# Half of two DRAM streams moved to GpSimd's queue, and a new order of the work, in a tuned Fourier filter with a gated convolution

## The chip, the cores and the metric

The kernel runs on one core of one Trainium2 chip. The metric is the device time in microseconds (us): the median of three runs is 857.64 us (857.32 to 858.21). The changed kernel is compared with the kernel before on the same chip. Inside the core, TensorE (PE in the profile) does the matrix products, VectorE (DVE) and ScalarE (ACT) do the element-wise work, SyncE (SP) issues nearly all transfers, and GpSimd (POOL) is almost unused before the change.

## The reference

```
x: (8, 3200, 256)
X  = rfft(x, axis=1)
Yr = X.real @ w_r - X.imag @ w_i + b_r
Yi = X.real @ w_i + X.imag @ w_r + b_i
Yr, Yi = soft-threshold of both by 0.01       # sign(Y) * max(|Y| - 0.01, 0)
y  = irfft(Yr + 1j*Yi, n=3200, axis=1)        # (8, 3200, 256)
gate_pre[s] = sum over k < 5 of conv_w[k] * y[s - 4 + k]   # causal, per channel
out = (sigmoid(gate_pre) * (y @ w_val)) @ w_out
```

The three convolution matrices (`moe_w_val`, `moe_conv_w`, `moe_w_out`) arrive as 64-bit floats or as 32-bit ones; here the kernel holds code that turns 64-bit words into 32-bit floats on VectorE.

## The kernel before, in words

The transform of 3200 points is split into 64 x 50 points, forwards and backwards. One batch (of eight) goes through five stages:

1. **p1**, the first transform: eight units `u`. A unit reads eight of the 64 columns of x as two halves of a tile (`half(0)`, rows 0 to 49, and `half(1)`, rows 64 to 113), makes four or five products into `p` (L594, L599, L601), copies one half to SBUF on ScalarE (L607) and makes sum and difference with the other half on VectorE (`fold`, L613). `store` writes the result `s` to the scratch `a_dram` in DRAM (L554 through `by_rows`, L631 for one column of unit 0).
2. **p2**: blocks `d` of four frequencies each are read back from `a_dram` (`a`, L650), transformed again (`s`, L668), split into high and low parts (`xs`, L713 to L721), multiplied with the complex weights (`y_ps`, L782 and L786, with the bias seed on ScalarE, L764, and a bias step on VectorE, L788, between the two), soft-thresholded (`tp`, L794 and L796), transformed back (`z_ps`, L737) and written to `z_dram` (L753).
3. **positions**: eight groups read `z_dram` (`zl`), make the last transform (`y_p`, L848) and put y into `y_sb`; when group 1 is there, a small copy (L866) joins the ends of the sequence.
4. **conv**: ScalarE makes the first tap (L896), VectorE the other four (`acc`, L899), ScalarE the sigmoid (L909).
5. **gated**: the value product (`v_ps`), the gating (L933), the output product (`o_ps`), and the store to `out` (L960). The big products are made of three matmuls on a high and a low part each (L882); the last ones of the run use whole 32-bit words instead (L878).

The stages of neighbouring batches overlap: p1 of batch b+1 runs beside p2 of batch b and the positions, conv and gated work of batch b-1. `a_dram` exists twice, so p2 of a batch starts only when all its stores have landed.

**What sets the order.** The program is not written in the order in which it runs. `Plan.add` collects pieces with an engine, a cost and a key `at`; `Plan.order` then plays them on one queue per engine and, among the pieces that could begin at about the same time, takes the one with the smallest `at`. The keys are `batch * 13 + unit` plus offsets from the table `O`, one offset per kind of piece. The planner knows transfers by their kilobytes only: one common wire of `WIRE` bytes per ns, a lag `LANDED` and a `BACKLOG`. The result is a fixed list of instructions for each engine. Every engine and every queue works its list strictly in order.

**Queues.** `QUEUES` names SyncE and ScalarE; ScalarE's queue is used only for one half of x in the first two units of batch 0. All else (1001 transfers in the list) is SyncE's. A transfer of 50 rows is issued as two (`ROWS`: 48 rows and 2 rows). A queue has eight completion counters that it uses in turn, so a transfer waits for the one eight places before it on the same queue.

**Idle TensorE.** Before real work is there, TensorE runs products that nobody reads (`warm`, L987, and `zeros`, L363).

## Time and profile before

| | |
|---|---|
| median of three runs | 857.64 us |
| the profiled execution's own time | 859.73 us |
| span from its first to its last instruction | 857.8 us |
| mean granted TensorE clock | 0.973 of full |
| PE busy | 821.0 us, 96% |
| DVE busy | 736.2 us, 86% |
| ACT busy | 593.7 us, 69% |
| POOL busy | 4.5 us, 1% |
| transfers | 162.27 MB in 125909 packets, mean 189 GB/s |

Busy shares are means over stages with different limits. TensorE's matmuls overlap, so a busy TensorE is not TensorE at its peak. In the rows further down a line begins with either a stretch of time or a source line; a value in square brackets, or behind a second bar, is idle time of the engine just before and what ended it. "PEclk" is the TensorE clock that was granted, as a share of its full speed, and "DMA share" the mean busy share of the 16 DMA engines. The first positions group of batch 0, which opens the steady part of the run, begins at 152.8 us.

### The profile page before, as it was taken

How to read it: one execution, taken by the hardware profiler on the slowest of the kernel's cores; microseconds unless marked ns; L12 is line 12 of the kernel's file. 1: busy time of each engine (PE TensorE's matmuls, PEld its weight loads, DVE VectorE, ACT ScalarE, POOL GpSimd, SP SyncE). 2: the span in 40 equal slices, each digit the busy share in tenths (PEclk: the TensorE clock that was granted, in tenths of full speed). 3: DMA queues.
4: the chain of work that ended last, by engine and by line, in shares of the span. 5: the costliest groups of instructions: out<-in, count | busy, mean ns of one | idle time of the engine just before them, and what ended most of it. 6: DMA issues, size and time to landing. Idle time of an engine off the chain costs nothing.

```text
span 857.8 us, 23810 instructions
## 1 busy us (share of the span) xinstructions
PE 821.0 (96%) x9866; PEld 700.7 (82%) x9866; DVE 736.2 (86%) x1006; ACT 593.7 (69%) x903; POOL 4.5 (1%) x12
## 2 busy tenths in 40 slices
PE   8878867999999999999999999999999999999997
PEld 2456656889888988889988989899888999998874
DVE  3345679799998999899989998999989998998795
ACT  2234635778777786778777886878777787776753
POOL 0000000000000000000000000000001000000000
PEclk7888979999999999999999999999999999999999
DMA  6688889867886569776796759876895576225422
GB/s 169 182 190 224 246 214 250 228 179 191 209 234 185 165 180 258 203 204 174 224 245 195 192 175 248 206 206 187 231 234 158 157 200 193 71 83 173 133 76 96
DMA packets 125909, 162.27 MB, mean 189 GB/s; under 512 B 12528, under 2 KB 100234, under 8 KB 125802
## 3 DMA queue, kind: packets, MB, share of 16 engines
q1 hardware_dynamic: 125598, 160.34, 68.1%
q8 instruction: 78, 1.28, 0.7%
q10 hardware_dynamic: 204, 0.41, 0.2%
q14 instruction: 29, 0.24, 0.1%
HBM read 82.06 MB, written 78.64 MB: 187 GB/s over the span
## 4 chain that ended last, share of the span: by engine, by line
PE 69%; DVE 13%; DMA 9%; ACT 4%; SPq 3%; issue 2%; DVEq 0%; ACTq 0%
PE o_ps L882 13%; PE y_ps L782 12%; PE v_ps L882 11%; PE y_p L848 10%; PE y_ps L786 6%; DMA x<-in_x 4%; PE p L594 4%; PE s L668 4%; PE z_ps L737 4%; DVE acc L899 4%; PE v_ps L878 2%; SPq L554 2%; DMA zl<-z_dram 1%; DVE acc L933 1%; DVE gated L390 1%
## 5 line engine op out<-in xcount | busy, mean ns | idle before, releaser
L899 DVE SCALAR_TENSOR_TENSOR acc<-y_sb,cw_sb,acc 128x800 f32<-128x800 f32 x256 | 263.0, 1047 | 16.1 <-ACT acc L896 15.6
L782 PEld LDWEIGHTS y_ps<-w_sb,xs 128*128 128x128 f32 x1152 | 144.3, 191 | 28.4 <-DVE y_ps L788 12.4
L782 PE MATMUL y_ps<-w_sb,xs 128*128 128x256 f32 x1152 | 156.3, 286 | 11.1 <-DVE y_ps L788 11.0
L882 PE MATMUL o_ps<-gated,wo_sb 128*128 128x400 f32 x744 | 150.8, 349 | 0.8 <-DVE gated L390 0.8
L882 PEld LDWEIGHTS o_ps<-gated,wo_sb 128*128 128x128 f32 x744 | 134.6, 188 | 4.1 <-DVE gated L390 1.1
L882 PE MATMUL v_ps<-y_hl,wv_sb 128*128 128x400 f32 x648 | 128.4, 346 | 0.5 <-DVE s L613 0.5
L882 PEld LDWEIGHTS v_ps<-y_hl,wv_sb 128*128 128x128 f32 x648 | 115.4, 188 | 1.1 <-PE y_ps L786 0.7
L613 DVE TENSOR_TENSOR s<-p,s 128x512 f32<-128x512 f32 (+2 forms) x144 | 89.3, 626 | 27.5 <-ACT s L607 16.4
L848 PEld LDWEIGHTS y_p<-g_sb,zl 100*64 100x64 f32 x2048 | 89.1, 137 | 11.7 <-ACT y_ps L764 3.5
L848 PE MATMUL y_p<-g_sb,zl 100*64 100x100 f32 x2048 | 97.4, 251 | 0.7 <-DMA zl<-z_dram 0.5
L786 PE MATMUL y_ps<-w_sb,xs 128*128 128x256 f32 x576 | 90.0, 293 | 7.6 <-ACT y_ps L764 7.6
L786 PEld LDWEIGHTS y_ps<-w_sb,xs 128*128 128x128 f32 x576 | 79.3, 194 | 20.9 <-ACT y_ps L764 9.0
L794 ACT ACTIVATE tp<-y_ps,nlam 128x512 f32<-128x512 f32 (+1 forms) x104 | 70.0, 674 | 25.1 <-PE y_ps L782 25.1
L388 ACT CAST gated<-acc 128x800 fp32r<-128x800 f32 x62 | 53.3, 859 | 30.7 <-DVE acc L933 30.5
L601 PE MATMUL p<-x,f_sb 50*64 50x512 f32 x240 | 72.2, 654 | 1.7 <-DMA x<-in_x 1.7
L933 DVE TENSOR_TENSOR acc<-v_ps,acc 128x800 f32<-128x800 f32 x64 | 62.9, 984 | 11.4 <-PE v_ps L878 5.5
L796 DVE SCALAR_TENSOR_TENSOR tp<-y_ps,tp 128x512 f32<-128x512 f32 (+1 forms) x104 | 68.6, 661 | 4.1 <-ACT tp L794 4.0
L594 PE MATMUL p<-x,f_sb 50*64 50x512 f32 x256 | 71.6, 647 | 0.1
L668 PEld LDWEIGHTS s<-f_sb,a 64*64 64x64 f32 x3072 | 53.7, 137 | 19.5 <-issue 11.6
L909 ACT ACTIVATE acc<-acc 128x800 f32<-128x800 f32 x64 | 55.8, 878 | 16.3 <-DVE acc L899 16.0
L958 ACT COPY o<-o_ps 128x800 f32<-128x800 f32 x63 | 51.8, 822 | 21.3 <-PE o_ps L882 15.8
L716 DVE TENSOR_TENSOR sx<-s,sx 128x512 f32<-128x512 f32 x48 | 33.0, 688 | 38.2 <-ACT xs L713 37.2
(92 smaller groups left out, 1031.3 us busy)
## 6 DMA issues: line engine op xcount, KB each, us to landing
out<-o SPq DMA_DIRECT2D x126, 200.0 KB
a<-a_dram SPq DMA_DIRECT2D x96, 256.0 KB
z_dram<-z_t SPq DMA_DIRECT2D x48, 512.0 KB
zl<-z_dram SPq DMA_DIRECT2D x64, 384.0 KB
a_dram<-s SPq DMA_DIRECT2D x120, 192.0 KB
x<-in_x SPq DMA_DIRECT2D x119, 192.0 KB
a_dram<-s SPq DMA_DIRECT2D x120, 8.0 KB
x<-in_x SPq DMA_DIRECT2D x119, 8.0 KB
```

The costliest lines, as they stand in the source:

```text
L594: nc.tensor.matmul(p[k * HP:(k + 1) * HP, 0, :], f1_sb[half(0), 0:HP], xt[half(0), k * 512:(k + 1) * 512], start=True, stop=True)
L601: nc.tensor.matmul(dst, f1_sb[half(1), 0:HP], back[:, 2 * k:2 * k + 2, :], start=True, stop=True)
L613: nc.vector.tensor_tensor(out=st()[lo:hi, h, n], in0=tl[kp][lo:hi, 0, n], in1=st()[lo:hi, 1, n], op=(ALU.add, ALU.subtract)[h])
L668: nc.tensor.matmul(p[e * HP:(e + 1) * HP, h, c, t, :], tl[ka][rows, t, c * P + e * HP:c * P + (e + 1) * HP], f2_sb[rows, (4 * d + t) * N1: ...
L782: nc.tensor.matmul(p[:, 1 - r, :], xm(hx, c, r, i), w_sb[:, m, hw, c, :], start=False, stop=k == 5, skip_group_check=True)
L786: nc.tensor.matmul(tl[ky][:, 0], sm(hx, c, i), w_sb[:, 0, hw, c, :], start=False, stop=k == 5, skip_group_check=True)
L794: nc.scalar.activation(out=buffer(kt, "tp", [P, 2, D])[:, 0:n], in_=tl[ky][:, 0:n], func=AF.Relu, bias=nlam)
L796: add(at + 0.2, "DVE", dve(n * D), lambda: nc.vector.scalar_tensor_tensor(out=tl[kt][:, 0:n], in0=tl[ky][:, 0:n], scalar=LAM, in1=tl[kt][: ...
L848: nc.tensor.matmul(dst[e * HP:(e + 1) * HP], zt[0:Q, m, c * P + e * HP:c * P + (e + 1) * HP], g, start=True, stop=True)
L882: nc.tensor.matmul(p[:, e, 0:TB], w[:, hw, c, e * P:(e + 1) * P], src(hy, c), start=n == 0, stop=n == 5)
L899: nc.vector.scalar_tensor_tensor(out=acc(c), in0=wide(c, j), scalar=cw_sb[:, c, j:j + 1], in1=acc(c), op0=ALU.mult, op1=ALU.add)
L933: add(at + O["gate"], "DVE", dve(2 * TB), lambda: nc.vector.tensor_tensor(out=part(), in0=by_half(tl[kv][:, :, 0:TB]), in1=part(), op=ALU. ...
```

## The change

Three things change together.

- **Queues.** `QUEUES` is now SyncE and GpSimd. In every unit of p1 of every batch, half 0 of x is loaded by SyncE and half 1 by GpSimd. `store` is cut into two pieces `k` of four columns each: piece 0 goes by SyncE and piece 1 by GpSimd, except in units 5 to 7 of batch 0, where both go by SyncE. SyncE's list shrinks from 1001 transfers to 717, GpSimd's grows from none to 274 (144 for x, 130 for `a_dram`), ScalarE's six go.
- **Layout.** A row of `a_dram` was one frequency of one fold (100 rows: first all sums, then all differences). Now a row is a frequency (50 rows) with the sum and the difference of each column side by side, and the SBUF tile `s` has the same order, so that a store moves rows of 1024 words in one piece where before it moved two runs of 512 words. The column of unit 0 that is written with its folds exchanged takes two transfers instead of four. The reads of `a` keep runs of 256 words.
- **Order.** The planner gets a model of the eight counters of a queue (`lanes`), other constants and a newly searched table `O`. Every engine's list is in a new order. The memsets on GpSimd that nobody needs at once are put behind the first ones.

```diff
+        lanes, turn = {e: [0.0] * 8 for e in (False, True)}, {False: 0, True: 0}
+        def lane(p):
+            row, at = lanes[p["engine"] == "POOL"], turn[p["engine"] == "POOL"]
+            return max([row[(at + j) % 8] - 350 * j for j in range(lanes_of(p))], default=0.0)
...
-WIRE = 250
+WIRE = 260
 BACKLOG = 5000
-LANDED = 2500
+LANDED = 2200
+SOFT = 1500
...
-     'p3': 1.0966,
-     'conv': 25.53,
+     'p3': 9.2044,
+     'conv': 42.5736,
...
-    QUEUES = (("SP", nc.sync), ("ACT", nc.scalar))
-    BOTH = 2
+    QUEUES = (("SP", nc.sync, 700), ("POOL", nc.gpsimd, 1040))
...
+        first = -100 + u if early else at + O["load_x"] + O["load_x_1"] * (b == 1)
+        for g, (eng, queue, cost) in enumerate(QUEUES):
+            add(first + 0.001 * g, eng, cost, lambda g=g, queue=queue: load(g, queue), (),
+                [kx + (g,)], None if g else {kx: x_tag}, kb=200, chain="x" + eng, extra=SOFT * g)
...
-        st = lambda: tl[ks].rearrange("p (h n) -> p h n", h=NH)
+        st = lambda: tl[ks].rearrange("p (m h c) -> p h m c", h=NH, c=D)
...
-        def store():
+        def store(k, queue):
+            if u == k == 0:
+                buffer(ka, "a_dram", [N2, NM * 2 * D])
+            lo = (2 * u + k) * 4 * D
+            n = 2 * D if lo == 0 else 0
+            by_rows(queue, tl[ka][:, lo + n:lo + 4 * D], tl[ks][k * HP:k * HP + N2, n:], rows)
             if u == 0:
-                buffer(ka, "a_dram", [Q, NM * D])
-            dst = tl[ka].rearrange("(h f) mc -> f h mc", h=NH)
-            for k in range(2):
-                lo = u * 4 * D + k * 512
-                n = D if lo == 0 else 0
-                by_rows(nc.sync, dst[:, :, lo + n:lo + 512], st()[k * HP:k * HP + N2, :, n:], rows)
-            if u == 0:
-                for g in range(NH):
-                    for r in range(2):
-                        nc.sync.dma_start(out=dst[r::2, g, 0:D], in_=st()[r:N2:2, 1 - g if r else g, 0:D])
+                both = lambda ap: ap.rearrange("f (h c) -> f h c", h=NH)
+                queue.dma_start(out=both(tl[ka][k::2, 0:2 * D]), in_=both(tl[ks][k:N2:2, 0:2 * D])[:, ::1 - 2 * k])
+        for k, (eng, queue, cost) in enumerate(QUEUES[:1] * 2 if early and u > 4 else QUEUES):
...
-            src = tl["a_dram", b].rearrange("(h f) (m c) -> h (f m) c", h=NH, c=D)
+            src = tl["a_dram", b].rearrange("f (m h c) -> h (f m) c", h=NH, c=D)
```

**Where the order changes, first place.** SyncE's list of the kernel before, from the last stores of batch 0 to the first read of `a` and what follows (`s1_254` is unit 7's folded tile, `x_296` unit 0 of batch 1; 1024 words are one row of a half):

```order
L554 DMA a_dram_168<-s1_254 48x2x512
L554 DMA a_dram_168<-s1_254 2x2x512
L490 DMA g1_sb_70<-in_g1 128x256
L650 DMA a_293<-a_dram_168 64x4x256 x2
L554 DMA x_296<-in_x 48x1024
L554 DMA x_296<-in_x 2x1024
L554 DMA x_296<-in_x 48x768
L554 DMA x_296<-in_x 2x768
```

SyncE's list of the changed kernel at the same place (`s1_253` is unit 7, `x_297` and `x_302` are units 1 and 2 of batch 1; unit 0 of batch 1 stands still earlier, ahead of all stores):

```order
L568 DMA a_dram_175<-s1_253 48x1024
L568 DMA a_dram_175<-s1_253 2x1024
L568 DMA x_297<-in_x 48x1024
L568 DMA x_297<-in_x 2x1024
L568 DMA x_302<-in_x 48x1024
L568 DMA x_302<-in_x 2x1024
L504 DMA g1_sb_70<-in_g1 128x256
L499 DMA f2_sb_68<-in_f2 128x256
L658 DMA a_309<-a_dram_175 64x4x256 x2
L658 DMA a_312<-a_dram_175 64x4x256 x2
```

Three units of batch 1's x and a further part of the matrix `f2` now stand ahead of the first read of `a`, and the second read follows the first at once. In GpSimd's list 18 transfers of batch 0's x (half 1 of eight units) and 11 stores (units 0 to 4) come before its three units of batch 1.

**Second place.** TensorE's list of the kernel before, around the point where VectorE turns `moe_w_val` into 32-bit words (`p_1042` is unit 0 of batch 2; the conversion's 13 VectorE instructions stand between that unit's folds and the bias step that releases the third row from the bottom):

```order
L786 MATMUL y_ps<-w_sb,xs 128x256 x6
L594 MATMUL p_1042<-x,f_sb 64x512 x2
L599 MATMUL p_1042<-x,f_sb 64x256 x2
L601 MATMUL p_1042<-x,f_sb 64x512
L782 MATMUL y_ps<-w_sb,xs 128x256 x12
L786 MATMUL y_ps<-w_sb,xs 128x256 x6
L782 MATMUL y_ps<-w_sb,xs 128x256 x12
L786 MATMUL y_ps<-w_sb,xs 128x256 x6
L737 MATMUL z_ps<-tp,g_sb 64x256 x8
```

TensorE's list of the changed kernel around the same conversion (`p_1061` and `p_1073` are units 0 and 1 of batch 2; the conversion stands before the bias step that releases the `x12` row under them):

```order
L794 MATMUL y_ps<-w_sb,xs 128x256 x6
L603 MATMUL p_1061<-x,f_sb 64x512 x2
L608 MATMUL p_1061<-x,f_sb 64x256 x2
L610 MATMUL p_1061<-x,f_sb 64x512
L603 MATMUL p_1073<-x,f_sb 64x512 x2
L610 MATMUL p_1073<-x,f_sb 64x512 x2
L790 MATMUL y_ps<-w_sb,xs 128x256 x12
L794 MATMUL y_ps<-w_sb,xs 128x256 x6
L745 MATMUL z_ps<-tp,g_sb 64x256 x8
```

Two units of p1 now stand between the sums and the product that waits for the conversion, and their folds come behind the conversion on VectorE and not ahead of it.

**In numbers, over the whole lists.** The count of matmuls that are used stays the same on every line; those that nobody reads fall from 26 to 22 (`zeros`), with 13 `warm` ones in both. TensorE goes between 64-column and full tiles 192 times before and 204 times after. Behind the last threshold step of the run (L796, now L804), VectorE has 42 taps, 13 gatings and 12 splits left before, and 56, 16 and 18 after. Behind the last `y_ps` product, TensorE has 36 more `v_ps`, 36 more `o_ps` matmuls and three more `y_p` groups left than before.

## Rows read from the trace of the kernel before

**Rows 1.** Busy time in stretches of the start, all engines (window, share; clock, DMA)
```profile
0.00:21.00 21.00, 17.59 (x54) 4.92 (x58) 7.68 (x13) 4.66 (x8) 1.29 (x10) 0.71 0.69 170
21.00:41.00 20.00, 19.56 (x84) 10.27 (x84) 8.23 (x14) 5.72 (x11) 0.00 (x0) 0.88 0.69 192
41.00:70.00 29.00, 20.25 (x306) 14.58 (x306) 12.69 (x21) 9.52 (x16) 0.00 (x0) 0.88 0.82 188
70.00:95.00 25.00, 21.90 (x265) 16.34 (x258) 13.82 (x21) 13.39 (x22) 0.00 (x0) 0.86 0.88 236
...
116.00:137.00 21.00, 20.61 (x276) 16.10 (x280) 16.49 (x41) 13.31 (x23) 0.00 (x0) 0.87 0.94 250
```

**Rows 2.** The same view of the steady part and of the end
```profile
153.00:753.00 600.00, 597.90 (x7833) 538.63 (x7830) 564.07 (x750) 467.65 (x711) 3.26 (x2) 1.00 0.72 197
...
774.00:858.00 84.00, 78.19 (x540) 60.10 (x538) 64.29 (x69) 47.03 (x61) 0.00 (x0) 0.98 0.38 116
```

**Rows 3.** TensorE's waits from 41 to 153 us (total us, times, longest)
```profile
PE y_ps L782 <- DVE y_ps L788: 11.0, 3, 7.6
PE y_ps L786 <- ACT y_ps L764: 6.6, 3, 4.5
PE s L668 <- DMA a<-a_dram: 5.0, 2, 4.2
PE s L668 <- DMA f_sb<-in_f: 2.5, 1, 2.5
```

**Rows 4.** Timeline of SyncE's queue (start, us, instructions)
```profile
1.56 16.09 SPq L554 DMA_DIRECT2D x<-in_x  x28
...
26.42 11.80 SPq L554 DMA_DIRECT2D a_dram<-s  x24
...
40.99 1.33 SPq L650 DMA_DIRECT2D a<-a_dram  x2
```

**Rows 5.** The chain that ended last, two transfers of the start (start, us)
```profile
17.02 3.17 DMA x<-in_x
...
37.56 3.37 DMA a_dram<-s
```

**Rows 6.** Issues of x by queue (ns: least, median, longest)
```profile
L554 SPq DMA_DIRECT2D x<-in_x x266: 231/310/1473, 1.6 to 642.4; - x133
...
L554 ACTq DMA_DIRECT2D x<-in_x x6: 288/336/599, 1.4 to 5.6; - x6
```

**Rows 7.** Timeline of GpSimd, the last of its opening memsets
```profile
1.73 0.14 POOL L503 MEMSET b_sb<- 1x63 f32 x1
```

**Rows 8.** Timeline around the conversion of moe_w_val, VectorE and TensorE
```profile
108.92 1.35 DVE L430 TENSOR_SCALAR st<-st 128x512 int32<-128x512 int32 x3
...
115.73 0.43 DVE L788 TENSOR_TENSOR y_ps<-y_ps,bias_sb 128x256 f32<-128x256 f32 x1
...
116.22 2.93 PE L782 MATMUL y_ps<-w_sb,xs 128*128 128x256 f32 x12 [7.65 <-DVE y_ps L788]
```

**Rows 9.** The chain that ended last, TensorE in the steady part
```profile
335.94 1.56 PE y_ps L782 x12
337.51 2.18 PE v_ps L882 x12
339.68 1.42 PE y_ps L782 x12
341.81 2.90 PE y_p L848 x64
```

**Rows 10.** Timeline beside GpSimd's only two large instructions, VectorE and GpSimd
```profile
650.94 1.98 POOL L969 TENSOR_TENSOR w_late<-wv_sb 128x512 f32<-128x512 f32 x1 [649.07 <-DVE y_hl L390]
...
653.16 1.89 DVE L899 SCALAR_TENSOR_TENSOR acc<-y_sb,cw_sb,acc 128x800 f32<-128x800 f32 x1
...
655.91 1.04 DVE L899 SCALAR_TENSOR_TENSOR acc<-y_sb,cw_sb,acc 128x800 f32<-128x800 f32 x1
```

**Rows 11.** Timeline of VectorE in the end, eight taps in a row
```profile
804.90 7.78 DVE L899 SCALAR_TENSOR_TENSOR acc<-y_sb,cw_sb,acc 128x800 f32<-128x800 f32 x8
```

More of the change, by code (lines that the diff above doesn't have):

```diff
@@ L208, in order @@
                 delay = wire - start + LANDED + p["extra"]
+                n = lanes_of(p)
+                for j in range(n):
+                    lanes[e == "POOL"][turn[e == "POOL"] % 8] = start + delay - p["kb"] * 1024 / WIRE * (n - 1 - j) / n
+                    turn[e == "POOL"] += 1
             free[e] = start + busy
@@ L272, with lanes_of @@
 FILL = 36000, 200000
-WIRE = 250
+WIRE = 260
 BACKLOG = 5000
-LANDED = 2500
+LANDED = 2200
+SOFT = 1500
+def lanes_of(p):
+    return max(1, round(p["busy"] / (520 if p["engine"] == "POOL" else 360))) if p["kb"] else 0
 def dve(n, copy=False):
@@ L291 @@
 T = float(NU)
-O = {'spread': -91.8948,
-     'hold': 1.0724,
-     'together': 1.2701,
-     'later': -3.6572,
-     'load_x': 9.9589,
-     'p1': 0.1254,
-     'p1_step': 1.2361,
-     'load_a': -5.3199,
-     's2': -1.7149,
-     's1i': 1.553,
-     'p3': 1.0966,
-     'load_z': -28.9681,
-     'y': 11.7985,
-     'conv': 25.53,
-     'val': 6.1049,
-     'gate': -22.7084,
-     'project': 7.8156,
+O = {'spread': -99.8597,
+     'hold': 2.2571,
+     'together': 0.8995,
+     'later': 26.9179,
+     'load_x': 17.5888,
+     'p1': 2.4323,
+     'p1_step': 0.8634,
+     'load_a': 10.0095,
+     's2': -2.3478,
+     's1i': 1.9676,
+     'p3': 9.2044,
+     'load_z': -0.8895,
+     'y': 0.9651,
+     'conv': 42.5736,
+     'val': 3.9538,
+     'gate': -29.4145,
+     'project': 5.3323,
      'late_val': 6.023,
      'late_out': 14.484,
-     'turn': -55.8644,
-     'pre': -4.984,
-     'mix_sum': -1.4205,
-     'p1_1': -7.3343,
-     'load_x_1': -7.2435,
-     'p1_2': -1.5627,
-     'p3_0': 0.9988}
+     'turn': -93.545,
+     'pre': -22.8171,
+     'mix_sum': -1.0816,
+     'p1_1': -0.3777,
+     'load_x_1': -45.5576,
+     'p1_2': -1.2032,
+     'p3_0': -2.8835}
 WARM = 2, 1, 1, 1, 8
@@ L571, in p1, with load @@
         rows = ROWS
-        def load(h):
-            xt = room(kx, x_tag, 4 * D) if h in (0, None) else tl[kx]
+        def load(g, eng):
+            xt = room(kx, x_tag, 4 * D) if g == 0 else tl[kx]
             src = x[b].rearrange("(n m) c -> n (m c)", m=N1)
-            for g in range(NH) if h is None else (h,):
-                eng = QUEUES[g][1] if early and u < BOTH else nc.sync
-                lo = (N1 - 3 - 4 * u if g else 4 * u) * D
-                n = 3 * D if g and u == 0 else 4 * D
-                by_rows(eng, xt[half(g), 0:n], src[:, lo:lo + n], rows)
-                if n < 4 * D:
-                    by_rows(eng, xt[half(g), n:], src[:, NM * D:(NM + 1) * D], rows)
-        if early:
-            for h in range(NH):
-                add(-100 + u, QUEUES[h][0] if u < BOTH else "SP", 650, lambda h=h: load(h), (), [kx + (h,)], None if h else {kx: x_tag}, kb=200)
-        else:
-            add(at + O["load_x"] + O["load_x_1"] * (b == 1), "SP", 1300, lambda: load(None), STORED if b == 1 else (),
-                [kx + (0,), kx + (1,)], {kx: x_tag}, kb=400, chain="x")
+            lo = (N1 - 3 - 4 * u if g else 4 * u) * D
+            n = 3 * D if g and u == 0 else 4 * D
+            by_rows(eng, xt[half(g), 0:n], src[:, lo:lo + n], rows)
+            if n < 4 * D:
+                by_rows(eng, xt[half(g), n:], src[:, NM * D:(NM + 1) * D], rows)
+        first = -100 + u if early else at + O["load_x"] + O["load_x_1"] * (b == 1)
+        for g, (eng, queue, cost) in enumerate(QUEUES):
+            add(first + 0.001 * g, eng, cost, lambda g=g, queue=queue: load(g, queue), (),
+                [kx + (g,)], None if g else {kx: x_tag}, kb=200, chain="x" + eng, extra=SOFT * g)
         def products():
@@ L602, in p1 @@
         add(at, "PE", 890, products, [kx + (0,), kx + (1,), ("f1", 0, 0)], [kp + (0,)] + ([("turn", "p1", u)] if early else []), {kp: p_tag}, mode="q")
[L603 removed]
+        st = lambda: tl[ks].rearrange("p (m h c) -> p h m c", h=NH, c=D)
         def keep():
             room(ks, s_tag, 1024)
[L607 removed]
+            nc.scalar.copy(out=st()[:, 1], in_=tl[kp][:, 1].rearrange("p (m c) -> p m c", c=D))
             if u == 0:
[L609 removed]
+                nc.scalar.copy(out=st()[0:HP, 0, 0], in_=tl[kp][0:HP, 0, 0:D])
         def fold(h):
[L612 to L613 removed]
+            p = tl[kp].rearrange("p g (m c) -> p g m c", c=D)
+            for lo, hi, n in ((0, P, slice(1, 2)), (HP, P, slice(0, 1))) if u == 0 else ((0, P, slice(0, 2)),):
+                nc.vector.tensor_tensor(out=st()[lo:hi, h, n], in0=p[lo:hi, 0, n], in1=st()[lo:hi, 1, n], op=(ALU.add, ALU.subtract)[h])
         end = early and u == 7
```

24 lines of the change are left out of this document (10 added, 14 removed).

## The prediction, written before the changed kernel ran

> **What bounds the kernel now.** I read the busy time in stretches first, then TensorE's waits, then the queue's timeline, and the chain that ended last only to price single steps. The stretches divide the run in three. From 153 to 753 us TensorE is busy 597.9 of 600 us at the full clock, and VectorE 564.1 of 600 [rows 2]: both are nearly full, and no transfer can be worth much there. In the first 153 us the picture is another one. TensorE shows 17.6 to 21.9 us of work in stretches of 20 to 29 us, but a part of that is work that nobody reads, the granted clock is 0.71 to 0.88 of full (a mix of the two levels), and the DMA share climbs from 0.69 to 0.94 [rows 1]. From 774 us to the end TensorE has 5.8 us idle and VectorE 19.7 us [rows 2]. So the start is where time can be found; the middle can only be kept, and the end can be lost.
>
> In the start the reader is to see two kinds of waits of TensorE [rows 3]: for transfers (5.0 us for `a`, 2.5 us for a part of `f2`) and for VectorE or ScalarE (11.0 and 6.6 us), of which the longest, 7.6 us, and another, 4.5 us, stand beside the conversions of 64-bit weights. Ahead of them lies a stretch in which TensorE has nothing to wait with: SyncE issues x until 17.7 us, the last of x lands at 20.2 us, 24 stores take 11.8 us of the queue until 38.2 us, the last lands at 40.9 us, and the first read of `a` is issued at 41.0 us [rows 4, 5].
>
> **The change part by part.** The sum is made against the profiled execution: 859.73 us, of which 857.8 are span. The median of the runs is 857.64 us, 2.09 us less, and the gain is taken off that.
>
> *Loading, storing and the first reads, 0 to 70 us.* By their rates these 70 us move 170 x 21 + 192 x 20 + 188 x 29 kB, so 3.57 + 3.84 + 5.45 = 12.9 MB, at a mean of 184 GB/s with DMA shares of 0.69, 0.69 and 0.82 [rows 1]. Later stretches move 236 and 250 GB/s at shares of 0.88 and 0.94 [rows 1], so the wires can carry more than the one queue feeds them. The change takes half of x and half of the stores off SyncE's list and gives them a second set of eight counters, and a store's row goes in one run instead of two. Nothing of the bytes goes away: three units of batch 1's x and a part of `f2` only come earlier. I take a rate between the old 184 and the later 236, 205 GB/s: 12.9 / 0.205 = 62.7 us, **7.3 us** gained. I don't take the first read of `a` itself to come much earlier than 41 us, since 1.3 MB more stand ahead of it; the gain is that p1 of these units and the second read are done when it comes. Bounds: at 240 GB/s (between the two later rows) it is 53.6 us, 16 us gained. GpSimd's price for issuing a transfer is not in the trace. The nearest rows are SyncE's, median 0.31 us and longest 1.473 us (with its wait in it), and ScalarE's, median 0.336 us [rows 6]. GpSimd's opening memsets end at 1.9 us [rows 7], and 18 loads and 11 stores follow before the last store of units 0 to 4 is out. At 0.336 us that is 1.9 + 29 x 0.336 = 11.6 us, far ahead of the folds that they wait for; at 1.473 us it is 44.6 us, and with 3.4 us to land 48.0 us, 7 us later than now. I take it nearer to the two medians, and keep -16 and +7 as the ends.
>
> The 2.5 us for `f2` lie in this stretch and go with it; they are not counted again.
>
> *The waits beside the conversions.* The conversion of `moe_w_val` holds VectorE from 108.9 to 115.7 us, and TensorE waits 7.65 us for the bias step behind it; the clock falls meanwhile, since the twelve matmuls after it take 2.93 us against 1.42 us in the steady part [rows 8, 9]. The conversions stay before the steady part in the new order. But now two units of p1 stand in TensorE's list inside this wait; a unit is four or five of the products, and TensorE's list also has the folds of the units behind the conversion. I take 2.5 us off this wait, and 1 us off the 4.5 us one, **3.5 us** in all. The bounds are 0 (the wait is only moved) and 8 us (both waits and the slow matmuls are mostly gone).
>
> *From 70 us to 153 us* the DMA share is high in the stretches shown, 0.88 and 0.94 [rows 1], so I give the second queue nothing more there: 0, bounds -5 and +3.
>
> *The middle.* TensorE changes between the two tile sizes 204 instead of 192 times. Twelve matmuls take 1.56 us behind small tiles and 1.42 us behind full ones [rows 9], so a change costs 0.14 us: 12 x 0.14 = **1.7 us** lost. x and stores of later batches move beside 0.72 DMA share [rows 2] and are due well before they are used; their cover is the whole batch before, and if it goes, TensorE waits for p1 in each of seven batches.
>
> *The end.* The new keys let p2 run further ahead of conv and gating. Behind the last threshold step VectorE has 14 taps, 3 gatings and 6 splits more; at 7.78 / 8 = 0.97 us for 800 columns [rows 11] that is 23 x 0.97 = 22.4 us. TensorE has 72 matmuls of 2.18 / 12 = 0.18 us and three groups of 1.45 us more [rows 9]: 13.1 + 4.4 = 17.5 us. So VectorE's remainder grows by 4.9 us more than TensorE's. VectorE has 19.7 us idle in the end now [rows 2], some 10 us of it behind its last gating, so half may be covered: **2.4 us** lost, bounds 0 and 5.
>
> Folds and copies that now write in steps of 256 columns are taken at their old time: the count of elements is the same.
>
> Sum: -7.3 - 3.5 + 0 + 1.7 + 2.4 = -6.7 us; 859.73 - 6.7 = 853.0 us for the profiled execution, and 857.64 - 6.7 = **850.9 us** for the median.
>
> **The rivals.**
>
> *The engines are the limit, not the queue* (no change). If 0.69 to 0.94 of DMA share is all that such small transfers can fill, the first term is 0 and the rest is -3.5 + 4.1 = +0.6 us: 858.2 us. For it: 0.82 between 41 and 70 us [rows 1] at only 188 GB/s, so a high share there moves little. Against it: 0.69 in the first 41 us, with SyncE's list issuing without a gap.
> The Trainium skill has this as a rule (DMA: Bandwidth & Descriptors, section Rules for kernel authors): transfers from SyncE, ScalarE and GpSimd run on the same 16 engines, and spreading them saves issue time only. By that rule this rival's 858.2 us would be the answer; the trace agrees for 116 to 137 us, at a share of 0.94, and not for the first 41 us, at 0.69.
>
> *GpSimd's queue is slow* (slower). Its transfers stand in one list, in order, and the reads of `a` need all stores. By the line above, the read slips to 1.9 + 29 n + 3.4 us for n us per transfer. The other terms sum to +0.6, so the kernel gets slower from where this passes 41 us, at n = 1.22 us; at the longest row, 1.473 us, the first term is +7 and the time 865.3 us. For it: no row shows this queue at all. Against it: two hardware queues show medians of a third of a us [rows 6].
>
> *GpSimd holds VectorE up* (slower). One tap took 1.89 us beside GpSimd's two large instructions and 1.04 us a little later [rows 10]: 0.85 us of delay for an instruction with two operands in SBUF. Some 200 of the 274 transfers fall behind 153 us, where VectorE has 36 us idle in 600 [rows 2]. From 36 / 200 = 0.18 us per transfer the slack is used up; at 0.25 us it is 14 us on top of the forecast, 865 us. Against it: the delayed tap stood beside an instruction that reads and writes 512 columns, not beside a transfer's issue.
> The Trainium skill (SBUF — State Buffer, section Who interferes with whom) says that VectorE instructions with two SBUF inputs collide with GpSimd instructions that read SBUF, not with those that only write. By that rule issuing costs VectorE nothing and the forecast stays at 850.9 us; the delayed tap agrees with its first half, and no row here shows the second.
>
> *The start is worth more* (faster). With 240 GB/s up to 70 us and both conversion waits mostly covered the sum is -16 - 6 + 4.1 = -17.9 us: 839.7 us. For it: the later stretches do reach such rates. Against it: they do so with more reads of `a` in flight than the start has.
>
> **How the numbers follow.** Forecast, 851 us: 0.50. Start worth more, about 840 us: 0.15. Engines the limit, about 858 us: 0.14. Slow queue, about 865 us: 0.14. VectorE held up, about 865 us or more: 0.07. The forecast's own range is 845 to 855.5 us. A measurement can tell about 0.2% from no change, so "same" is 855.9 to 859.4 us. Faster: 0.50 + 0.15 and a little of the third case, 0.66. Same: 0.13. Slower: 0.21. The range 840 to 862 us leaves out about 0.07 below and 0.12 above.
>
> **What would show it.** Right: the first `y_p` comes near 143 us instead of 152.8; the stretch 0 to 70 us moves 200 GB/s or more; the wait of `y_ps` for the bias step shrinks from 7.65 to some 5 us; the steady part has 600 us of TensorE as full as before; VectorE's taps keep 0.97 us each; the last 84 us have less VectorE idle time. Wrong: a chain in the start that runs through GpSimd's queue, a first read of `a` later than 43 us, taps longer than 1.1 us beside GpSimd's transfers, or waits of TensorE for x in the middle. If the gain comes from the middle or from the end, my reading of where the time lies is wrong even if the total fits.

## The result, and the profile after it

The changed kernel takes 843.92 us (median of 4 runs, 842.51 to 846.47) beside 857.84 us for the kernel before on the same chip: a ratio of 0.9842, 95% interval 0.9817 to 0.9866, or 13.9 us less. The forecast was 850.9 us. The time lies just below the forecast's own range (845 to 855.5 us) and above the rival "the start is worth more" (839.7 us).

The profiled execution took 846.47 us, of which 844.7 are span; its mean clock is 0.978. First the busy time in stretches, as in [rows 1, 2]. The columns are the window, its length, and the busy time of TensorE, its weight loads, VectorE, ScalarE and GpSimd with their counts; then the granted clock, the DMA share and GB/s.

```profile
0.00:21.00 21.00, 16.24 (x49) 5.07 (x50) 5.49 (x10) 4.36 (x8) 12.07 (x31) 0.76 0.86 178
21.00:41.00 20.00, 16.52 (x76) 7.79 (x77) 11.09 (x19) 6.78 (x14) 10.03 (x19) 0.98 0.86 251
41.00:70.00 29.00, 26.50 (x349) 20.49 (x350) 16.80 (x26) 12.47 (x20) 9.11 (x17) 0.84 1.02 248
70.00:95.00 25.00, 25.00 (x393) 19.91 (x396) 18.45 (x32) 17.50 (x29) 7.59 (x15) 1.00 0.85 225
...
116.00:137.00 21.00, 18.63 (x287) 14.91 (x286) 16.78 (x31) 11.71 (x23) 4.37 (x8) 0.86 0.96 246
153.00:753.00 600.00, 598.73 (x7645) 533.40 (x7639) 557.76 (x744) 464.37 (x703) 95.80 (x177) 1.00 0.69 194
761.00:845.00 84.00, 78.71 (x537) 62.02 (x535) 72.27 (x78) 48.27 (x63) 0.00 (x0) 0.98 0.32 99
```

Between 21 and 70 us the chip now moves 250 GB/s where it moved 190 [rows 1] (the view's share can come out above 1). From 70 to 95 us TensorE has no idle time left (25.00 of 25), against 21.90 before. The steady part is as busy as before on TensorE; VectorE works 6.3 us less in it than in [rows 2], and 8.0 us more in the last 84 us, where its idle time fell from 19.7 us to 11.7.

TensorE's waits from 0 to 153 us (total, times, longest), to be set against [rows 3]:

```profile
PE y_ps L790 <- DVE y_ps L796: 4.6, 2, 4.3
PE p L603 <- DMA x<-in_x: 3.5, 1, 3.5
PE p L608 <- issue: 2.8, 1, 2.8
PE y_ps L794 <- ACT y_ps L772: 2.4, 1, 2.4
PE z_ps L739 <- DVE xs L725: 1.9, 1, 1.9
PE s L676 <- DMA f_sb<-in_f: 1.7, 1, 1.7
...
PE s L676 <- DMA a<-a_dram: 0.6, 1, 0.6
```

The two waits beside the conversions, the longest of their rows, fell from 7.6 and 4.5 us to 4.3 and 2.4 (the rows' totals from 11.0 and 6.6 to 4.6 and 2.4), and the one for `a` from 5.0 to 0.6 us. Both waits beside the conversions are still there. Two others have grown in these 153 us: for x from 1.7 to 3.5 us and for `xs` from 0.2 to 1.9. SyncE's timeline, against [rows 4]:

```profile
1.57 8.34 SPq L568 DMA_DIRECT2D x<-in_x  x16
...
22.86 13.17 SPq L568 DMA_DIRECT2D a_dram<-s  x18
...
39.44 2.67 SPq L658 DMA_DIRECT2D a<-a_dram  x4
```

And GpSimd's, which had no transfer before (in brackets its idle time and what ended it):

```profile
1.83 4.34 POOL L568 DMA_DIRECT2D x<-in_x  x8
6.55 1.15 POOL L568 DMA_DIRECT2D x<-in_x  x2 [0.38 <-DMA x<-in_x]
8.64 0.54 POOL L568 DMA_DIRECT2D x<-in_x  x1 [0.95 <-DMA x<-in_x]
9.64 0.52 POOL L568 DMA_DIRECT2D x<-in_x  x1 [0.45 <-DMA x<-in_x]
```

Eight transfers go out in a row, and from the ninth on GpSimd waits until one of its own has landed: in this program a queue has eight counters, and the ninth transfer needs the first one's. Their size makes no difference: where GpSimd issues transfers of two rows alone (the run with small pieces below), it stops behind the eighth as well:

```profile
1.83 4.29 POOL L554 DMA_DIRECT2D x<-in_x  x8
6.97 0.52 POOL L554 DMA_DIRECT2D x<-in_x  x1 [0.84 <-DMA x<-in_x]
```

SyncE's row in [rows 4] can be read the same way: 28 issues of 0.31 us [rows 6] are 8.7 of its 16.09 us, and most of the rest is waiting for its own x. This is the wait in the trace of the kernel before, up to 45 us (total, times, longest):

```profile
SPq L554 <- DMA x<-in_x: 6.6, 9, 1.8
```

What GpSimd pays for an issue (ns: least, median, longest), and what VectorE's taps take beside it:

```profile
L568 POOL DMA_DIRECT2D x<-in_x x144: 512/523/757, 1.8 to 606.5; - x144
L568 POOL DMA_DIRECT2D a_dram<-s x122: 512/522/604, 18.9 to 632.3; - x122
```
```profile
L907 DVE SCALAR_TENSOR_TENSOR acc<-y_sb,cw_sb,acc 128x800 f32<-128x800 f32 x256 | 259.7, 1043 | 7.3 <-ACT acc L904 6.1
L907 DVE SCALAR_TENSOR_TENSOR acc<-y_sb,cw_sb,acc x256: 1035/1043/1054, 152.9 to 830.5; 128x800 f32<-128x800 f32 x128
```

0.52 us per transfer, and a mean tap of 1043 ns; it was 1047 ns before. The longest of the 256 taps takes 1054 ns, so none is held up.

### The profile page after: what moved, and what is told of

The parts are those of the page before. It is cut to its first block, busy times and chain, and to the rows that moved or that the text cites. A ratio compares the mean times of both kernels' runs of the same rounds, so it can differ in the third digit from the quotient of the medians.

```text
span 844.7 us, 24140 instructions
## 1 busy us (share of the span) xinstructions
PE 819.1 (97%) x9858; PEld 696.6 (82%) x9858; DVE 737.0 (87%) x1006; ACT 595.7 (71%) x903; POOL 150.4 (18%) x286
## 4 chain that ended last, share of the span: by engine, by line
PE 72%; DVE 19%; DMA 4%; ACT 2%; issue 2%; SPq 1%; POOL 0%; ACTq 0%; DVEq 0%; POOLq 0%
PE y_ps L790 14%; PE o_ps L890 11%; PE v_ps L890 11%; PE y_p L856 9%; PE y_ps L794 8%; DVE acc L907 7%; PE s L676 5%; PE z_ps L745 5%; PE p L603 5%; DVE acc L941 2%; DVE gated L404 2%; DVE s L623 1%; DVE y_hl L404 1%; DMA a<-a_dram 1%; ACT xs L721 1%
## 5 line engine op out<-in xcount | busy, mean ns | idle before, releaser
L907 DVE SCALAR_TENSOR_TENSOR acc<-y_sb,cw_sb,acc 128x800 f32<-128x800 f32 x256 | 259.7, 1043 | 7.3 <-ACT acc L904 6.1
L890 PEld LDWEIGHTS o_ps<-gated,wo_sb 128*128 128x128 f32 x744 | 132.0, 188 | 8.6 <-ACT sx L717 2.3
L568 POOL DMA_DIRECT2D x<-in_x x144 | 76.6, 537 | 317.9 <-PE p L610 301.0
L856 PEld LDWEIGHTS y_p<-g_sb,zl 100*64 100x64 f32 x2048 | 89.5, 137 | 16.5 <-issue 7.2
L856 PE MATMUL y_p<-g_sb,zl 100*64 100x100 f32 x2048 | 100.9, 252 | 0.0
L568 POOL DMA_DIRECT2D a_dram<-s x122 | 64.0, 529 | 165.6 <-DVE s L623 129.2
L804 DVE SCALAR_TENSOR_TENSOR tp<-y_ps,tp 128x512 f32<-128x512 f32 (+1 forms) x104 | 68.8, 662 | 8.4 <-ACT tp L802 7.7
L603 PE MATMUL p<-x,f_sb 50*64 50x512 f32 x256 | 72.4, 651 | 3.5 <-DMA x<-in_x 3.5
L610 PE MATMUL p<-x,f_sb 50*64 50x512 f32 x240 | 73.1, 657 | 0.5 <-DMA x<-in_x 0.5
L772 ACT COPY y_ps<-bias_sb 128x256 f32<-128x256 f32 x104 | 39.5, 381 | 35.2 <-DVE tp L804 31.5
```

Source lines behind the costliest of these rows:

```text
L568: eng.dma_start(out=out[lo:hi], in_=in_[lo:hi])
L603: nc.tensor.matmul(p[k * HP:(k + 1) * HP, 0, :], f1_sb[half(0), 0:HP], xt[half(0), k * 512:(k + 1) * 512], start=True, stop=True)
L610: nc.tensor.matmul(dst, f1_sb[half(1), 0:HP], back[:, 2 * k:2 * k + 2, :], start=True, stop=True)
L804: add(at + 0.2, "DVE", dve(n * D), lambda: nc.vector.scalar_tensor_tensor(out=tl[kt][:, 0:n], in0=tl[ky][:, 0:n], scalar=LAM, in1=tl[kt][: ...
L856: nc.tensor.matmul(dst[e * HP:(e + 1) * HP], zt[0:Q, m, c * P + e * HP:c * P + (e + 1) * HP], g, start=True, stop=True)
L890: nc.tensor.matmul(p[:, e, 0:TB], w[:, hw, c, e * P:(e + 1) * P], src(hy, c), start=n == 0, stop=n == 5)
```

## The experiments

Theory A: the second queue in the start is the gain. Rivals: the new order (B) or the layout (C) is. The first four kernels take the three parts of the change apart. Each figure below is the median beside that of the kernel before in the same comparison, with the ratio's 95% interval.

**One queue.** The changed kernel, with every transfer on SyncE's list:

```diff
-    QUEUES = (("SP", nc.sync, 700), ("POOL", nc.gpsimd, 1040))
+    QUEUES = (("SP", nc.sync, 700), ("POOL", nc.sync, 1040))
```

> The changed kernel with only the second queue undone: SyncE issues GpSimd's transfers too, at the places that they had in the written order; TensorE, VectorE and ScalarE run the same lists as in the changed kernel. Theory A (the second queue in the start is the gain): 854 to 858 us, the first y_p back after 148 us, 0 to 70 us back below 200 GB/s. Rival B (the new order of the engines is the gain): 844 to 849 us, the first y_p before 138 us. Rival C (the long rows in DRAM are the gain): as B, with a_dram's stores landing sooner than before.

852.26 us beside 858.29, ratio 0.9935 (0.992 to 0.995): 6.0 us of the 13.9 are left, between A and B. 8 us belong to the queue, not all. Up to 70 us the chip moves 200 GB/s. The sign that I had named for A fails, though: the first y_p comes at 140.8 us. A part of that is its place in TensorE's list: by the traces' counts 8 matmuls of p, 32 of s, 6 of y_ps and 16 of z_ps, which stood ahead of the first y_p in the old order, stand behind it in the new one, some 3 us of work by the prices given further down (an estimate). The time of a first instruction compares two starts only where the order is the same.

**Layout alone**, on the kernel before:

```diff
-        st = lambda: tl[ks].rearrange("p (h n) -> p h n", h=NH)
+        st = lambda: tl[ks].rearrange("p (m h c) -> p h m c", h=NH, c=D)
...
-                buffer(ka, "a_dram", [Q, NM * D])
+                buffer(ka, "a_dram", [N2, NM * 2 * D])
...
-                by_rows(nc.sync, dst[:, :, lo + n:lo + 512], st()[k * HP:k * HP + N2, :, n:], rows)
+                by_rows(nc.sync, tl[ka][:, lo + n:lo + 4 * D], tl[ks][k * HP:k * HP + N2, n:], rows)
```

> The kernel before with only the new layout of a_dram (both folds side by side, a store's row in one run, two transfers instead of four for the first unit's own columns); old order, SyncE alone. Theory A: 855 to 858 us, first y_p at 150 to 153 us, since the stores end behind the folds either way. Rival C (the layout is the gain): 847 to 851 us, the stores' landing to the first read of a at least 3 us shorter.

854.48 us beside 858.29, ratio 0.9956 (0.9941 to 0.9972): 3.8 us, between the two forecasts. SyncE's timeline:

```profile
26.10 10.32 SPq L554 DMA_DIRECT2D a_dram<-s  x24
...
38.84 1.33 SPq L650 DMA_DIRECT2D a<-a_dram  x2
```

The 24 stores take 10.32 us instead of 11.80 and the first read of `a` is issued 2.15 us earlier [rows 4]. A row in one run is worth something when one queue is all there is: 3.8 us by the medians.

**Queue alone**, on the kernel before:

```diff
-                eng = QUEUES[g][1] if early and u < BOTH else nc.sync
+                eng = nc.gpsimd if g else nc.sync
...
-                by_rows(nc.sync, dst[:, :, lo + n:lo + 512], ...
+                by_rows(nc.gpsimd if k and not (early and u > 4) else nc.sync, dst[:, :, lo + n:lo + 512], ...
```

(and the two transfers with odd rows of unit 0's own column).

> The kernel before with only the second queue: half 1 of every unit's x and the second piece of every store go by GpSimd, but for the stores of units 5 to 7 of batch 0; old layout, and TensorE, VectorE and ScalarE keep the order of before. Theory A: 846 to 851 us, first y_p at 138 to 146 us, over 210 GB/s in the first 70 us. Rival B (the order is the gain): 854 to 858 us. Rival D (the queue and an order planned for it are only worth something together): 856 us or more, with waits for x or a in the start.

849.21 us beside 858.29, ratio 0.9902 (0.9883 to 0.992): 9.1 us with every engine's old order, as A had it. The start in one row, and SyncE's first read of `a`:

```profile
0.00:70.00 70.00, 63.71 (x564) 34.59 (x564) 33.89 (x56) 25.16 (x44) 33.50 (x70) 0.85 0.91 228
```
```profile
36.42 1.35 SPq L650 DMA_DIRECT2D a<-a_dram  x2
```

228 GB/s up to 70 us, where the kernel before moved 184; the read is 4.6 us earlier. The conversions' waits are untouched: 7.7 and 4.5 us in their longest.

**Old layout** in the changed kernel (the layout's edit the other way round):

> The changed kernel with only the layout undone (a_dram in two halves, each row of a store in two runs, four transfers for the first unit's own columns); new order and both queues. Theory A: 844 to 847 us, first y_p at 133 to 135 us. Rival C (the layout is the gain): 850 to 856 us, more packets and a later first read of a.

845.31 us beside 858.29, ratio 0.9861 (0.984 to 0.9882). Beside the changed kernel's interval that is no difference: with two queues the layout gives nothing that can be measured. C falls.

**Queue and layout in the old order** (the two edits above together):

> The kernel before with the second queue and the new layout, without the new order: TensorE, VectorE and ScalarE work in the order of before. Alone the queue gave -9.1 us and the layout -3.8 us. Theory A2 (the queue and the layout are two cures of one ailment, stores too slow ahead of the first read of a; the order brings 3 to 4 us of its own by covering the conversions): 846 to 849 us, and the waits of 7.7 and 4.5 us beside the conversions are still there. Rival E (the two add up, the order brings nothing): 843 to 845.5 us.

848.49 us beside 857.75, ratio 0.9886 (0.9863 to 0.9908): 9.3 us, no more than the queue alone. Queue and layout are two cures of one ailment, and rival E falls. Where the gain lies can be read from the first y_p, since these kernels have one order: it comes at 152.8 us before, at 142.6 with the queue and at 143.3 with both, and from there to the end of the span all three take the same 705.0, 705.0 and 704.8 us. So all of it lies in front of the first y_p. The remaining 4.6 us come with the order.

**GpSimd in the start only.** The changed kernel, with SyncE for batches 2 to 7:

```diff
-            add(first + 0.001 * g, eng, cost, lambda g=g, queue=queue: load(g, queue), ...
+            add(first + 0.001 * g, eng, cost, lambda g=g, queue=queue if b < 2 else nc.sync: load(g, queue), ...
```

(and the same in the stores).

> The changed kernel with GpSimd's queue for the x and stores of batches 0 and 1 only; from batch 2 SyncE issues all of them, at the same planned places. If the queue is worth something in the start alone: within 1.5 us of the changed kernel, 842.5 to 846 us. If it also keeps the middle fed: 849 us or more, with waits of TensorE for x or for a after 200 us. If GpSimd's issuing costs VectorE something: 840 us or less, with shorter taps.

843.15 us beside 857.75, ratio 0.9832 (0.9805 to 0.9859): as the changed kernel. The queue earns all of it in the first two batches, and its issues later cost VectorE nothing (the mean tap is 1043 ns here too).

**Small pieces only.** The kernel before; GpSimd takes the two-row transfers alone:

```diff
-            eng.dma_start(out=out[lo:hi], in_=in_[lo:hi])
+            (nc.gpsimd if hi - lo == N2 - 48 else eng).dma_start(out=out[lo:hi], in_=in_[lo:hi])
```

> The kernel before with only the two-row transfers of x and of a_dram (8 KB, half of the transfers, 4% of the bytes) issued by GpSimd; the 48-row ones stay with SyncE. If the number of transfers on SyncE's list is the limit (its issue time and its counters): 848 to 851 us, as with the queue alone (849.2), and first y_p near 142 us. If the bytes of one queue are the limit (what a single queue can pull): 856 to 859 us, no change. In between if a two-row transfer is late on GpSimd's queue.

849.90 us beside 857.75, ratio 0.9903 (0.9887 to 0.992): 7.9 us, nearly what the whole queue gives, for 4% of the bytes. SyncE's timeline:

```profile
1.57 11.00 SPq L554 DMA_DIRECT2D x<-in_x  x14
...
23.90 9.44 SPq L554 DMA_DIRECT2D a_dram<-s  x12
...
36.34 1.35 SPq L650 DMA_DIRECT2D a<-a_dram  x2
```

So it is not bytes that one queue lacks: SyncE moves 96% of them still. What the 8 KB transfers took from SyncE was time on its list and places among its eight under way; the run does not say which of the two counts.

**Whole pieces.** Is the number of transfers alone the cause? The kernel before with one transfer of 50 rows instead of 48 and 2:

```diff
-    ROWS = ((0, 48), (48, N2))
+    ROWS = ((0, N2),)
```

> The kernel before, SyncE alone, with x and the stores in transfers of 50 rows instead of 48 and 2: half as many transfers, the same bytes, the same order. If the number of transfers on one list is the limit (theory A3, from the run in which the two-row ones alone went by GpSimd, -7.9 us): 849 to 853 us without any second queue, and the stores before the first read of a take 10 us or less of SyncE's list instead of 11.8. If 48 rows are taken because 50 sit unevenly on the 16 DMA engines, and this costs more than the number: 857 us or more, with longer landings. If GpSimd's queue gives something that fewer transfers do not: 854 to 857 us.

855.35 us beside 857.52, ratio 0.9973 (0.9961 to 0.9985): 2.2 us, which by the number alone is the third case: GpSimd's queue gives something that fewer transfers do not. SyncE's list, then the DMA share of its first 41 us in 40 slices (tenths) with what was moved, and the same two lines of the kernel before:

```profile
1.57 11.04 SPq L554 DMA_DIRECT2D x<-in_x  x14
...
24.85 11.10 SPq L554 DMA_DIRECT2D a_dram<-s  x12
...
39.95 1.35 SPq L650 DMA_DIRECT2D a<-a_dram  x2
```
```profile
DMA  0045666666666666666642688866666665665610
DMA packets 3857, 7.41 MB, mean 181 GB/s; under 512 B 436, under 2 KB 1556, under 8 KB 3856
...
DMA  0069648993999987563571158797977898866871
DMA packets 4119, 7.42 MB, mean 181 GB/s; under 512 B 699, under 2 KB 1817, under 8 KB 4117
```

The loads leave SyncE's list as fast as in the run before (11.04 against 11.00 us), but the share stands flat at 0.6 and the stores take 11.10 us for 12. A flat 0.6 would fit about ten of the 16 DMA engines at work all the time (0.6 x 16, an estimate; no row names the engines). The bytes moved in these 41 us are the same as before, and so is the rate; it does not rise as it does with a second queue. So this run changes how the transfers lie on the engines together with their number, and cannot tell what the number alone is worth. Nor do the runs separate the time of an issue from the place among eight.

**All stores split.** The changed kernel, with units 5 to 7 of batch 0 split as well:

```diff
-            add(at + 0.02 + 0.001 * k, eng, cost, lambda k=k, queue=queue: store(k, queue), ...
+            add(at + 0.02 + 0.001 * k, eng, cost, lambda k=k: store(k, QUEUES[k][1]), ...
```

> The changed kernel with the second piece of the stores of units 5 to 7 of batch 0 on GpSimd's queue as well, where SyncE has 18 store transfers in a row now (13.2 us) and GpSimd's list is empty. If SyncE's list ahead of the first read of a (issued at 39.4 us) is what sets that read: it is issued 3 us earlier, 36 to 37 us, and the time falls by 1 to 3 us to 841 to 843 us. If the wires or GpSimd's longer way set it: 843 to 846 us, read at 39 us or later.

846.94 us beside 857.75, ratio 0.9865 (0.9839 to 0.989): no gain, and a little above its second case. The first read is issued at 38.76 us, 0.7 us earlier. From the start of the long row of stores to the read it is 13.8 us (from 24.99) where it was 16.6 (from 22.86): SyncE's list is shorter, but the stores began later in this execution. Between executions of one list the read moves as much: in the run with GpSimd in the start only, whose start is the changed kernel's, it is issued at 37.23 us. So what sets the read is not shown; that the shorter list wins no time is.

**Without conversions.** What does the order bring? Both orders, with queue and layout, leave out 12 of the 13 steps of each conversion:

```diff
-            op("d", "m", 2.0 ** -20, ALU.mult, 1.0, ALU.add),
+            op("d", "hi", 2.0 ** -20, ALU.mult, 1.0, ALU.add),
...
-                fn()
+                if k == 7:
+                    fn()
```

> Queue and layout with the order of before (848.5 us), leaving out 12 of the 13 steps of each conversion of 64-bit weights (the weights of the two projections and of the convolution are then not the reference's). If the waits beside the conversions (7.6 and 4.5 us) are what the new order covers: 838 to 842 us, and the gap to the changed kernel with the same left out is under 2 us. If the order's 4.6 us come from elsewhere: both fall alike, and the gap stays at 4 to 5 us.

> The changed kernel (843.9 us), leaving out the same 12 steps of each conversion. If the new order covers the conversions: 839 to 842 us, within 2 us of the old order with the same left out. If not: it falls as far as the old order does, to 836 to 838 us, and stays 4 to 5 us ahead of it.

Old order: 840.86 us beside 857.52, ratio 0.9807 (0.9786 to 0.9828), 7.6 us less than with conversions (6.8 by the two ratios). New order: 845.68 us, ratio 0.986 (0.984 to 0.988), no less than with them. The conversions cost the old order some 7 us and the new one nothing that can be measured. The stretch from 70 to 153 us, in which they lie: the old order with conversions,

```profile
70.00:153.00 83.00, 66.86 (x971) 54.03 (x970) 61.68 (x119) 47.43 (x81) 21.25 (x40) 0.92 0.87 235
```

the new order with them,

```profile
70.00:153.00 83.00, 74.42 (x1141) 59.95 (x1144) 65.55 (x125) 53.49 (x90) 23.39 (x44) 0.92 0.94 243
```

and the old order without them:

```profile
70.00:153.00 83.00, 73.53 (x1127) 59.78 (x1126) 55.63 (x91) 54.89 (x93) 24.24 (x46) 0.96 0.96 260
```

TensorE works 66.9, 74.4 and 73.5 of 83 us: in this stretch the new order gives back what the conversions took. It does not do so by hiding the whole wait. With the conversions 4.3 and 2.4 us of waiting stand beside them; without them TensorE waits elsewhere in the first 153 us, for ScalarE in place of 2.4 us and for `a` in place of 0.6 us:

```profile
PE y_ps L795 <- ACT y_ps L773: 5.2, 3, 2.6
PE s L677 <- DMA a<-a_dram: 5.1, 6, 1.3
```

I had expected the two orders to meet; instead the new one is 4.8 us slower without conversions (the intervals do not overlap). The steady part in the old order and in the new, both without conversions:

```profile
153.00:753.00 600.00, 597.88 (x7637) 540.43 (x7630) 566.76 (x753) 466.88 (x708) 93.41 (x173) 1.00 0.68 191
```
```profile
153.00:753.00 600.00, 598.71 (x7650) 533.50 (x7644) 557.90 (x745) 463.87 (x702) 95.26 (x177) 1.00 0.70 194
```

TensorE is busy for 598 us in both, and 8.9 us of VectorE's work lie elsewhere in the new order. Busy time does not tell who is ahead; counts do, roughly. From 200 to 700 us the old order's trace has 111 matmuls of y_p more and 33 of v_ps and o_ps, and 36 of y_ps fewer. At 2.90 / 64, 2.18 / 12 and 1.42 / 12 us each [rows 9] these are 5.0 + 6.0 - 4.3 = 6.7 us. Of the other groups it has 8 p, 16 z_ps and 128 s fewer, some 3.9 us by an estimate from their spacing in the trace (0.11, 0.06 and 0.016 us each). So the old order gains some 3 us in these 500. The rest is there before them: at 70 us the old order's trace is ahead by 16 p, 64 s and 6 y_ps, at 200 us by 12 p, 12 v_ps and 1 o_ps, some 3.5 us each time by the same prices; behind 700 us it loses about 1 us again. But in the first 70 us, where no conversion lies yet, the granted clock was 0.98 in the old order's execution and 0.85 in the new one's. Executions of one start differ as much there (0.98 in the run with GpSimd in the start only, 0.85 in the changed kernel), so the first part need not be the order's.

The same tally of counts times prices can be made for every trace (estimates, all of them). From 70 to 153 us TensorE does 54 to 57 us of this work in the six traces of the old order with conversions and 64 without; in the new order it does 62 to 65 in the five with them and one queue or two, and 65 without. From 200 to 700 us it does 482.7 to 483.8 us in the seven traces of the old order and 479.9 to 481.3 in six of the new: the new order loses some 2.5 us in the middle, conversions or not.

**An earlier third phase.** Is it the changes of tile size (counted here between p or y_p and any other matmul)? The changed kernel with one key of the old table:

```diff
-     'p3': 9.2044,
+     'p3': 1.0966,
...
-     'p3_0': -2.8835}
+     'p3_0': 5.2243}
```

> The changed kernel with the third phase's key of before (p3 1.0966 instead of 9.2044, and p3_0 raised by the difference, 5.2243 instead of -2.8835, so that batch 0's own third phase starts where it did). TensorE's list is the same up to some 170 us; behind it the changes between p or y_p and other matmuls fall from 196 to 168, the number of the kernel before. Without conversions the new order was 4.8 us slower than the old one, with its start no worse. Theory F (the new table's late third phase costs this in the middle, by tile-size changes): 840 to 842 us, with a start like that of the changed kernel and more of VectorE's work done from 153 to 753 us. Rival G (the middle's price has another source): 843 to 845 us. Rival H (the late third phase pays in the end): 846 us or more, with more idle time of TensorE behind 760 us.

887.16 us beside 857.67, ratio 1.0338 (1.0321 to 1.0355). By the letter this is rival H's forecast, 846 us or more with more idle time in the end; but it is 43 us above the changed kernel, where H was meant to explain a few. Two stretches of this kernel, and then the first of them in the changed one:

```profile
300.00:400.00 100.00, 96.03 (x1205) 83.62 (x1198) 92.79 (x124) 73.28 (x111) 18.66 (x35) 0.98 0.72 198
...
820.00:887.00 67.00, 51.45 (x315) 36.71 (x312) 44.96 (x47) 29.69 (x36) 0.00 (x0) 0.92 0.23 73
```
```profile
300.00:400.00 100.00, 100.00 (x1251) 89.27 (x1250) 94.77 (x128) 79.29 (x120) 19.68 (x37) 1.00 0.75 211
```

It has as few changes of tile size as the kernel before, and TensorE is idle for 4 us in 100 here and for 15.6 of the last 67 (5.3 of the last 67 in the changed kernel). F and G fall. H is not shown either, since TensorE is idle in the middle too, of which H says nothing: what the key upset costs ten times what it was to win back, so the run says nothing of the price of a tile-size change. The keys of one table hang together, and one cannot be put back alone. What costs the new order its 2.5 us in the middle, and what it loses ahead of 70 us, stays open.

## Why the prediction was right in direction and too small

**The start, -7.3 us: the mechanism was right, the size low.** Queue and layout alone give 9.3 us. I took 205 GB/s up to 70 us; the old order with the queue reaches 228, and with the layout too 217. The reason that I gave holds: the wires could carry more than one list fed them. One reading beside it was wrong: SyncE's list did not issue "without a gap" but waited 6.6 us for its own x. What the list lacked was room for more transfers, not for bytes; whether issue time or the places among eight, no run separates.

**GpSimd's price: the choice between the bounds was right.** 0.52 us lies between the medians of 0.31 and 0.34 [rows 6] and the end of 1.473. By the prediction's own line the 29 transfers would be out at 1.9 + 29 x 0.52 = 17 us. That line left the waits for landings out. In the trace the last of the 18 loads goes out at 16.5 us and the last of the 11 stores is out at 25.8 us, and the first two stores wait 1.9 us for GpSimd's own x, so this list is not far ahead of the folds:

```profile
16.52 0.52 POOL L568 DMA_DIRECT2D x<-in_x  x1 [0.15 <-issue]
18.94 1.05 POOL L568 DMA_DIRECT2D a_dram<-s  x2 [1.90 <-DMA x<-in_x]
...
21.60 4.15 POOL L568 DMA_DIRECT2D a_dram<-s  x8
```

**The first read of `a`** comes at 39.44 us, not "much earlier than 41", as I took it. In the old order the queue alone brings it to 36.4 us. In the new one x of batch 1 stands ahead of it, as the prediction said; but in another execution of the same start it comes at 37.2 us, so how much that costs no run shows.

**The conversions' waits, -3.5 us: this step failed in size.** I took 2.5 us off one wait and 1 us off another. The two waits lost 3.3 and 2.1 us, the rows that they stand in 10.6 us together, and by the pair of runs without conversions these cost some 7 us in the old order and none that can be measured in the new. My bound of -8 was the answer. I had counted units of p1 in one wait as the only cover. How the new order does better is not shown in full: 6.7 us of waiting still stand beside the conversions, and without them other waits come in their place.

**70 to 153 us, 0:** for the queue that holds, since the run with the queue alone has its gain by 70 us. But the conversions' term falls due here: 74.4 us of TensorE's work in 83 instead of 66.9 with queue and layout in the old order.

**The middle, +1.7 us: the size is about right, the reason not shown.** By the counts the new order loses some 2.5 us between 200 and 700 us, with the conversions or without. I ascribed it to changes of tile size at 0.14 us each; the run that was to take them away upset more than it removed, so that the size fits may be luck.

**The end, +2.4 us: wrong.** I expected VectorE's longer remainder to be half covered. TensorE is busy for 78.7 of the last 84 us where it was 78.2, and the 8 us more of VectorE's work fit into its idle time. By the counts and prices above, what is left at 700 us even ends some 1 us sooner in the new order (its time is 23.9 us above its priced work, 25.1 in the kernel before).

Put together by the runs: -9.3 for queue and layout and -4.6 for the order, -13.9 us; the forecast had -7.3 and -3.5 + 1.7 + 2.4 = +0.6, -6.7 in all. Most of the miss is the order's. Its -4.6 can be split into -9.4 for the conversions (7.6, and 1.8 that the new order seems to lose without them, which is within its spread) and +4.8 for what it loses without them; these add up by the way they are formed and so check nothing. Each difference of two runs here is uncertain by some 2 us.

**The rivals.** "The engines are the limit" falls: 250 GB/s with the same bytes. The Trainium skill's rule beside it (DMA: Bandwidth & Descriptors, Rules for kernel authors), that spreading over queues does not help bandwidth and saves issue time only, differs from these runs in its first half: with the same bytes the second queue alone raises the rate up to 70 us from 184 to 228 GB/s and takes 9.1 us off. That the two-row transfers alone bring 7.9 of the 9.1 us would fit its second half, but saved places among the eight fit as well. "GpSimd's queue is slow" falls with 0.52 us. "GpSimd holds VectorE up" falls: a mean tap of 1043 ns beside 274 transfers, none above 1054, and no gain from taking them away after batch 1. That agrees with the Trainium skill (SBUF — State Buffer, Who interferes with whom), by which a VectorE instruction with two SBUF inputs collides with GpSimd instructions that read SBUF, not with those that only write it. "The start is worth more" named the right places, but put 16 us on the start, where 9.3 were measured with queue and layout.

**What was to be seen.** 0 to 70 us at 200 GB/s or more: 228. The bias step's wait at some 5 us: 4.3. Taps unchanged: yes. Less idle time of VectorE in the end: yes. The first y_p near 143 us: 133, but that sign is worth little, as the run with one queue showed. "The steady part as full as before" came true, but 598 busy of 600 us cannot show a loss of a few. One of the signs of being wrong was there too: the chain that ended last does begin in GpSimd's queue (start, us).

```profile
1.88 2.74 POOL x L568 x5
4.62 7.44 DMA x<-in_x
```

These are five issues at 0.54 us and the landing of the fifth. So GpSimd's price does stand on the path at first, with 2.7 us, while the whole is faster all the same; the sign was too coarse. None of the other three signs showed: the first read comes before 43 us, no tap is longer than 1.1 us, and from 153 to 753 us TensorE has no wait for x.

## What to carry to other kernels

Before giving a queue less to move, count its transfers: in this program a list with eight under way waits for the first to land, be it 8 KB or 192 KB, so sending the small remainders through an idle engine's queue can bring most of what a second queue brings (7.9 of 9.1 us here). Fewer and larger transfers need not do the same: they brought 2.2 us. Look for what one engine's long block makes others wait for, and price it by leaving the block out in both orders; the difference of the two is what the new order saves on the block, and the rows of waits tell whether it is covered or other waits stand in its place. In a stretch where an engine is busy all the time, compare orders by the work done, not by the busy time. Look at several executions of a list before reading one start against another.

## What the hardware showed beyond that

- GpSimd issues a transfer of 48 x 1024 or of 2 x 1024 elements in the same 0.52 us, and a store of the old layout, with two runs to a row, in 0.59 us (the run with the queue alone); SyncE's median over both sizes is 0.31 us [rows 6]. GpSimd's x land 5.1 us after their issue, its stores 4.4 us (medians).
- In the first 41 us transfers of 50 rows move 181 GB/s at a flat DMA share of 0.6 (mean 0.58); 48 and 2 rows apart move the same 181 GB/s at a share of 0.69 [rows 1].
- Executions of the same list differ by up to 4 us (842.5 to 846.5 us), and so do their starts: the profiled execution of the run with GpSimd in the start only moves 241 GB/s up to 70 us and has a span of 840.5 us, at a median that is the same as the changed kernel's.
